# Strassen's seven half products in place of eight for six pairs of blocks in the channel MLP's second batch

## The chip, the cores and the metric

The kernel runs on 1 core of one Trainium2 chip. The metric is the device time of one execution in microseconds (us). Engines are named as in the profile: PE (TensorE matmul) and PEld (its weight loads), DVE (VectorE), ACT (ScalarE), POOL (GpSimd), SP (the queue that issues most DMAs).

## What is computed

Hash-masked attention, a gated convolution block and a last block that mixes with two Fourier transforms and ends in a channel MLP. The change is in that MLP, shown here with the lines around it:

```
X = np.fft.fft(x, axis=1)
X = np.fft.fft(X, axis=2)
mixed = np.real(X).astype(np.float32)
u = x + mixed
mu = np.mean(u, axis=-1, keepdims=True)
var = np.mean((u - mu) ** 2, axis=-1, keepdims=True)
un = (u - mu) / np.sqrt(var + 1e-06)
ch = np.maximum(un @ w_ch1, 0.0) @ w_ch2
return (u + ch).astype(np.float32)
```

There are 2 batches of 768 tokens, 512 channels and 2048 hidden units. All is float32, and w_ch1 and w_ch2 come as float64.

## The kernel before

A float32 product is made of three products on PE: each operand is split into a high and a low part (type F32R), and high x high, low x high and high x low are summed in PSUM. The kernel runs attention, value product, mixing and channel MLP one behind the other; the change is in the last, function channel.

The 2048 hidden units are 16 blocks of 128 units. Step g of the loop (L1398) handles block f = g % 16 of batch g // 16. `first` (L1362) is the first product of a step: 4 chunks of channels x 3 products, over 512 and then over 256 tokens of the 768 (24 matmuls), into PSUM tile pf, of which there are two; behind each of the two pieces ACT writes the ReLU as the high part of `hidden` (L1374) and DVE the low part (L1375). `second` (L1377) multiplies the block's hidden units with its rows of w_ch2: 3 matmuls over 512 channels for each of the 6 tiles of 128 tokens, 18 in all, added up over all blocks in six PSUM tiles acc. Step g runs first(g) and then second(g - 1), so that ACT and DVE work on the hidden units of g meanwhile. `hidden` has two buffers, for even and odd blocks. In the first batch the steps also load and split the weights of later blocks (channel_split); all weights then stay in SBUF as wch[f], four tiles a block: high and low of w_ch1, high and low of w_ch2. In the second batch nothing is loaded, and POOL has no work. The centred tokens of the second batch lie transposed in uth and utl (high and low, 4 chunks of 128 channels x 768 tokens). At steps with 9 <= f < 15 ACT adds the mean back to one tile of u (L1413, 128x512). `result` (L1384) adds u to acc times rstd on DVE and sends the output from SP.

All engines take their instructions in the order in which the code is written (manual_schedule); pools reuse tiles with waits for the last use of each tile.

Of the kernel before, what the change touches and what calls it, by code (L numbers as in the profile page):

```python
# [10 lines left out]
F32 = mybir.dt.float32  # L11
F32R = mybir.dt.float32r
AF = mybir.ActivationFunctionType
ALU = mybir.AluOpType
# [3 lines left out]
P = 128  # L18
B, H, S, D = 2, 8, 768, 64
DM = H * D  # L20
DFF = 2048
NF = DFF // P
# [3 lines left out]
NC = DM // P  # L26
HS = S // 2
# [77 lines left out]
def block_kernel(  # L105
# [4 lines left out]
    nc = tc.nc  # L110

    def f32(ap):
        return ap.bitcast(F32)
# [10 lines left out]
    def pool(es, name, bufs=1, psum=False, side=None):  # L124
        kw = dict(space=bass.MemoryType.PSUM) if psum else {}
        if side:
            kw["side"] = side
        return es.enter_context(tc.tile_pool(name=name, bufs=bufs, reuse_waits="tile", **kw))
# [47 lines left out]
    def run(steps):  # L176
        for x in steps:
            x()
# [5 lines left out]
    g = [gpool.tile([P, NC, S + 1], F32, name=f"g{b}") for b in range(B)]  # L184
# [788 lines left out]
    with ExitStack() as es:  # L973
        ps, late, convs = attention(es)


    u, mu, uth, utl, rstd = [], [], [], [], []
    wq, wch, wraw, wst, wnext = None, [], {}, [], []

    def late_tiles():  # L980
        lpool = pool(ctx, "lpool", side="right")
        for b in range(B):
            u.append(lpool.tile([P, 6, DM], F32, name=f"u{b}"))
            mu.append(lpool.tile([P, 6, 2], F32, name=f"mu{b}"))
        rstd.append(lpool.tile([P, B, 6], F32, name="rstd"))
        uth.append(lpool.tile([P, NC, S], F32R, name="uth"))
        utl.append(lpool.tile([P, NC, S], F32R, name="utl"))

        nonlocal wq
        wq = pool(ctx, "wq", side="right")  # L990
        wst.append(pool(ctx, "wst", 2, side="right"))
        wch.append(channel_tiles(wq, 0))

    def channel_tiles(pl, f):
        return [pl.tile([P, NC, P] if i < 2 else [P, DM], F32R, name=f"w{i}_{f}") for i in range(4)]

    def channel_load(h):

        if h >= 2 * NF:
            return  # L1000
        f, i = divmod(h, 2)
        fs = slice(f * P, (f + 1) * P)
        r = wraw[h] = wq.tile([P, DM], I64, tag=f"raw{i}", name="raw")
        if i:
            nc.sync.dma_start(r, w_ch2[fs, :])
        else:
            nc.sync.dma_start(r.rearrange("p (c f) -> p c f", c=NC), w_ch1[:, fs].rearrange("(c p) f -> p c f", p=P))
# [4 lines left out]
    def channel_steps(h, spare=True):  # L1012
        f, i = divmod(h, 2)
        return from64(channel_words, wraw[h], lambda: wch[f][2 * i : 2 * i + 2], spare=spare)

    def channel_split(h):
        if h < 2 * NF:
            f, i = divmod(h, 2)
            run(channel_steps(h))
            channel_load(h + 2)  # L1020

    def center(b, t):

        st = wst[0].tile([P, 6], F32, tag="st", name="st")
        nc.vector.bn_stats(st, u[b][:, t, :])
        nc.vector.bn_aggr(mu[b][:, t, :], st)
        nc.vector.tensor_scalar(u[b][:, t, :], u[b][:, t, :], mu[b][:, t, 0:1], None, op0=ALU.subtract)

    def spread():
        r = rstd[0]  # L1030
        for b in range(B):
            nc.vector.tensor_scalar(r[:, b, :], mu[b][:, :, 1], 1e-6, None, op0=ALU.add)
        nc.scalar.activation(r, r, AF.Sqrt)
        nc.vector.reciprocal(r, r)

    def u_transpose(b, t, psum):
        pu = psum()
        for c in range(NC):
            nc.tensor.transpose(pu[:, c * P : (c + 1) * P], u[b][:, t, c * P : (c + 1) * P], ident)
        ts_ = slice(t * P, (t + 1) * P)  # L1040
        pv_ = pu.rearrange("p (c t) -> p c t", c=NC)
        nc.scalar.copy(uth[0][:, :, ts_], pv_)
        nc.vector.tensor_tensor(utl[0][:, :, ts_], pv_, f32(uth[0])[:, :, ts_], op=ALU.subtract)
# [299 lines left out]
    def channel(es):  # L1343
        fp = pool(es, "fp")
        psh = pool(es, "psh", 2, psum=True)
        psa = pool(es, "psa", psum=True)
        wch.extend([None] * (NF - 1))
        order = list(range(NF - 1, NF - 5, -1)) + list(range(1, NF - 4))
        for f in order[:4]:
            wch[f] = channel_tiles(fp, f)  # L1350
        hidden = [[fp.tile([P, S], F32R, name=f"hid{n}{i}") for i in range(2)] for n in range(2)]

        for f in order[4:]:
            wch[f] = channel_tiles(fp, f)
        run(wnext)
        channel_load(4)

        def tile_f():
            return psh.tile([P, 512], F32, tag="pf", name="pf")

        def tile_a(t):
            return psa.tile([P, 512], F32, tag=f"acc{t}", name="acc")  # L1362

        def first(g, a):
            f, (hh, hl) = g % NF, hidden[g % 2]
            w1h, w1l = wch[f][:2]
            cs = WIDE[a]
            pf = (tile_a(2 + a) if g == 1 else tile_f())[:, : cs.stop - cs.start]
            n = 0
            for w, x in ((w1h, uth[0]), (w1l, uth[0]), (w1h, utl[0])):  # L1370
                for c in range(NC):
                    nc.tensor.matmul(pf, w[:, c, :], x[:, c, cs], start=n == 0, stop=n == 3 * NC - 1)  # L1372
                    n += 1
            nc.scalar.activation(hh[:, cs], pf, AF.Relu)  # L1374
            nc.vector.scalar_tensor_tensor(hl[:, cs], pf, 0.0, f32(hh)[:, cs], op0=ALU.max, op1=ALU.subtract)  # L1375

        def second(g, t, acc):  # L1377
            f, (hh, hl) = g % NF, hidden[g % 2]
            w2h, w2l = wch[f][2:]
            ts_ = slice(t * P, (t + 1) * P)  # L1380
            for n, (x, w) in enumerate(((hh, w2h), (hh, w2l), (hl, w2h))):
                nc.tensor.matmul(acc, x[:, ts_], w, start=f == 0 and n == 0, stop=f == NF - 1 and n == 2)  # L1382

        def result(b, t, acc):  # L1384

            if t < 3:
                o = wq.tile([P, DM], F32, tag="cv" + "aeg"[t], name="o")
            else:
                if t != 4:
                    both[:] = [wq.tile([P, 2, DM], F32, tag=f"raw{t // 5}", name="o")]  # L1390
                o = both[0][:, t % 2, :]
            nc.vector.scalar_tensor_tensor(
                o, acc, rstd[0][:, b, t : t + 1], u[b][:, t, :], op0=ALU.mult, op1=ALU.add
            )
            nc.sync.dma_start(out[b, t * P : (t + 1) * P, :], o)

        both = []

        last = [tile_a(t) for t in range(2)]
        for g in range(B * NF + 1):  # L1400
            if g < B * NF:
                for a in range(2):
                    first(g, a)
                channel_split(2 * g + 3 if g != 1 else 4)
            if 4 <= g < 10:
                center(1, g - 4)
            elif g == 12:
                spread()
            if g > 0:
                b, f = divmod(g - 1, NF)  # L1410
                if 9 <= f < 15:
                    x = u[b][:, f - 9, :]
                    nc.scalar.activation(x, x, AF.Identity, bias=mu[b][:, f - 9, 0:1])  # L1413
                if f == 0:
                    acc = (last if b == 0 else [tile_a(t) for t in range(2)]) + [tile_a(t) for t in range(2, 6)]
                for t in range(6):
                    if g == NF - 1:
                        for x in ((), (0, 1), (2,), (3,), (4,), (5,))[t]:
                            u_transpose(1, x, tile_f)
                    second(g - 1, t, acc[t])  # L1420
                    if t == 2:
                        channel_split(2 * g + 4 if g > 1 else 5)
                    elif t == 5 and g == 1:
                        channel_split(6)
                    if f == NF - 1:
                        result(b, t, acc[t])

    with ExitStack() as es:
        channel(es)
# [35 lines left out]
```

## Time and profile before

| what | us |
|---|---|
| median of 3 runs | 611.06 (610.6 to 614.76) |
| the profiled execution | 610.95 |
| its span, first to last instruction | 609.1 |
| mean granted clock of TensorE | 0.999 of full speed |

The profile comes from one execution. A busy PE is not a PE at its peak, since the ends of matmuls are modelled and overlap the next start; the pace of PE is read from starts. A number such as L1372 is a line of the kernel before; the code of the change has lines of its own.

### The profile page before, as it was taken

The page shows a single profiled execution, that of the slowest core. Times are in us where ns is not written, and L with a number is a line of the kernel's source. Part 1 is how long each engine was busy: PE and PEld are TensorE (multiplying, and loading weights), DVE is VectorE, ACT ScalarE, POOL GpSimd, SP SyncE. Part 2 cuts the span into 40 slices and gives each one's busy share as a digit, 9 for nine tenths or more (in the row PEclk, how much of TensorE's full clock was granted, in tenths as well). Part 3 has the DMA queues.
Part 4 walks back from the last instruction along what each step waited for, and adds up shares of the span by engine and source line. Part 5 has one row for each costly group of instructions (what it writes and reads, how often), then busy time and mean ns, then how long its engine had stood idle before and what let it go on. Part 6 is the DMA issues. An engine that isn't in the chain of part 4 may idle for free.

```text
span 609.1 us, 10268 instructions
## 1 busy us (share of the span) xinstructions
PE 600.7 (99%) x3711; PEld 537.5 (88%) x3711; DVE 441.4 (72%) x849; ACT 357.7 (59%) x712; POOL 265.3 (44%) x274
## 2 busy tenths in 40 slices
PE   8999999999999999999999999999999999999997
PEld 7899999999999999998989888888888888888885
DVE  4999999999999997998679788988884411110113
ACT  5989999999999997745524455555665011111121
POOL 7251769788888798963341532332330000000000
PEclk9999999999999999999999999999999999999999
DMA  5967776878777712170200243443430200000002
GB/s 133 213 154 165 170 147 164 179 167 189 165 177 178 173 43 57 43 293 2 70 1 9 86 126 127 138 120 123 139 103 1 104 0 1 1 0 1 0 1 104
DMA packets 52556, 62.01 MB, mean 102 GB/s; under 512 B 28704, under 2 KB 39304, under 8 KB 52250
## 3 DMA queue, kind: packets, MB, share of 16 engines
q1 hardware_dynamic: 51770, 57.81, 37.3%
q0 software_dynamic: 432, 3.55, 1.5%
q8 instruction: 29, 0.48, 0.3%
q14 instruction: 21, 0.17, 0.1%
q10 hardware_dynamic: 304, 0.01, 0.0%
HBM read 36.73 MB, written 3.19 MB: 66 GB/s over the span
## 4 chain that ended last, share of the span: by engine, by line
PE 90%; DVE 6%; ACT 2%; issue 1%; DMA 1%; POOL 0%; SPq 0%; ACTq 0%; POOLq 0%
PE pf L1372 21%; PE acc L1382 20%; PE op L629 10%; PE sp L570 10%; PE ptp L606 9%; PE ps L1189 5%; PE ps L222 3%; PE ps L1253 3%; PE ps L1224 1%; PE bp L456 1%; PE late L222 1%; PE ptp L714 1%; PE early L222 1%; DVE ptl L618 1%; PE idle L369 1%
## 5 line engine op out<-in xcount | busy, mean ns | idle before, releaser
L1382 PE MATMUL acc<-w,hid 128*128 128x512 f32 x576 | 137.4, 391 | 0.0
L1382 PEld LDWEIGHTS acc<-w,hid 128*128 128x128 f32 x576 | 105.5, 188 | 20.1
L1375 DVE SCALAR_TENSOR_TENSOR hid<-pf,hid 128x512 fp32r<-128x512 f32 (+1 forms) x62 | 33.4, 556 | 120.6 <-ACT hid L1374 120.6
L1372 PE MATMUL pf<-uth,w 128*128 128x512 f32 (+1 forms) x496 | 97.2, 337 | 0.1
L1374 ACT ACTIVATE hid<-pf 128x512 fp32r<-128x512 f32 (+1 forms) x62 | 28.9, 488 | 114.9 <-PE pf L1372 114.9
L581 DVE TENSOR_SCALAR_CACHE_REDUCE sd<-sp 128x768 f32<-128x768 f32 x96 | 91.0, 948 | 4.8 <-PE sp L570 3.1
L618 DVE TENSOR_TENSOR ptl<-ptp,pth 128x768 fp32r<-128x768 f32 x96 | 91.5, 953 | 2.3 <-ACT pth L614 2.0
L570 PE MATMUL sp<-qk 128*128 128x512 f32 (+1 forms) x384 | 91.1, 359 | 1.7 <-DVE sd L581 0.8
L1372 PEld LDWEIGHTS pf<-uth,w 128*128 128x128 f32 x496 | 78.8, 188 | 15.6 <-DVE hid L1375 1.8
L588 ACT ACTIVATE sd<-sd,nm 128x768 f32<-128x768 f32 x96 | 90.5, 942 | 1.5 <-DVE sd L581 1.5
L614 ACT CAST pth<-ptp 128x768 fp32r<-128x768 f32 x96 | 77.4, 806 | 13.6 <-PE ptp L714 5.7
L162 POOL TENSOR_TENSOR w<-cv 128x512 fp32r<-128x512 f32 x31 | 40.4, 1302 | 89.0 <-DVE cv L157 74.5
L606 PE MATMUL ptp<-ident,sd 128*128 128x128 f32 x576 | 78.5, 272 | 0.2 <-ACT sd L588 0.2
L629 PE MATMUL op<-ptl,v 128*128 128x256 f32 x288 | 73.3, 284 | 0.2 <-DVE ptl L618 0.2
L629 PE MATMUL op<-pth,v 128*128 128x256 f32 x288 | 73.3, 282 | 0.0
L606 PEld LDWEIGHTS ptp<-ident,sd 128*128 128x128 f32 x576 | 65.8, 140 | 1.1 <-ACT sd L588 0.5
L570 PEld LDWEIGHTS sp<-qk 128*128 128x128 f32 x384 | 58.2, 189 | 8.3 <-DVE sd L581 1.6
L629 PEld LDWEIGHTS op<-pth,v 128*128 128x128 f32 x288 | 54.1, 188 | 4.1
L629 PEld LDWEIGHTS op<-ptl,v 128*128 128x128 f32 x288 | 54.1, 188 | 0.6 <-DVE ptl L618 0.4
L1372 PE MATMUL pf<-utl,w 128*128 128x512 f32 (+1 forms) x248 | 53.1, 335 | 0.0
L241 POOL TENSOR_TENSOR g<-g,conv_tmp 128x768 f32<-128x768 f32 x27 | 46.5, 1723 | 1.6
L149 ACT ACTIVATE cv<-cv,col 128x512 int32<-128x512 int32 x32 | 23.2, 725 | 40.4 <-DVE cv L146 40.4
(214 smaller groups left out, 984.2 us busy)
## 6 DMA issues: line engine op xcount, KB each, us to landing
raw<-in_moe_w_ch_dram SPq DMA_DIRECT2D x32, 512.0 KB
qk<-ht SPq DMA_DIRECT2D x60, 192.0 KB
qk<-lt SPq DMA_DIRECT2D x30, 192.0 KB
rqk<-in_q_dram SPq DMA_DIRECT2D x16, 192.0 KB
rqk<-in_k_dram SPq DMA_DIRECT2D x16, 192.0 KB
rv<-in_v_dram SPq DMA_DIRECT2D x8, 384.0 KB
out_dram<-o SPq DMA_DIRECT2D x12, 256.0 KB
xm<-xc SPq DMA_DIRECT2D x15, 192.0 KB
```

Source lines behind the costliest of these rows:

```text
L162: nc.gpsimd.tensor_tensor(dst()[1], fold(g.bitcast(F32)), fold(e.bitcast(F32)), op=ALU.mult)
L241: nc.gpsimd.tensor_tensor(dst, dst, tmp, op=ALU.add)
L570: nc.tensor.matmul(sp[:, cs], q2[i][:, m, qi * P : (qi + 1) * P], k2[i][:, m, cs], start=m == order[0], stop=m == order[1])
L581: nc.vector.tensor_scalar(sd[n], sp, CLAMP, None, op0=ALU.min, op1=ALU.min, accum_out=st[p]["nm"][:, n % 12 : n % 12 + 1],)
L588: nc.scalar.activation(sd[n], sd[n], AF.Exp, bias=st[p]["nm"][:, i : i + 1], scale=-1.0, accum_out=st[p]["sums"][:, i : i + 1],)
L606: nc.tensor.transpose(tp[:, r // 3, c0 : c0 + P], sd[n][:, r * P : (r + 1) * P], ident)
L614: nc.scalar.copy(p_parts(n)[0], tp)
L618: nc.vector.tensor_tensor(lo, tp, f32(ho), op=ALU.subtract)
L629: nc.tensor.matmul(po[kb], v3[:, r, c0 : c0 + P], pt[kb][x][:, r, :], start=r == 0 and x == 0, stop=r == R - 1 and x == 1,)
L1372: nc.tensor.matmul(pf, w[:, c, :], x[:, c, cs], start=n == 0, stop=n == 3 * NC - 1)
L1375: nc.vector.scalar_tensor_tensor(hl[:, cs], pf, 0.0, f32(hh)[:, cs], op0=ALU.max, op1=ALU.subtract)
L1382: nc.tensor.matmul(acc, x[:, ts_], w, start=f == 0 and n == 0, stop=f == NF - 1 and n == 2)
```

## The change

Steps 0 to 19 (the first batch and blocks 0 to 3 of the second) keep first and second. Then come six pairs of blocks, q = 2 to 7, with blocks 2q (e) and 2q + 1 (o). The first product of a pair is a 2x2 matrix product of halves: block e or o, upper or lower half of the channels (2 chunks of 128), left or right half of the tokens (384). Eight products of halves become seven (P1 to P7 in the order in which `seven` runs them), each of 6 matmuls of 384 tokens, of sums of weights and sums of tokens. The sums of tokens are made once (token_sums, DVE and ACT, in steps 17 to 19; tiles from batch 0's u, from raw0 and raw1 and from weight tiles no longer needed). The sums of weights are made for each pair (weight_sums, POOL and ACT), into the w_ch1 tiles of the pair two earlier. The seven products are added up in a new SBUF tile `between` (parts m, t1, t2), by one copy on ACT and seven additions on DVE, and four ReLU pieces of 384 tokens follow on ACT and four low parts on DVE. The second products of the pair before (two blocks, 36 matmuls) run between the products. The additions of the mean move behind seven(4) to seven(6), two tiles a time.

```diff
+        between = fp.tile([P, 3, HS], F32, name="between")
...
+        def token_sums(step):
...
+        def sum_tiles(q):
+            return [wch[f][i] for f in (2 * q - 4, 2 * q - 3) for i in range(2)]
+
+        def weight_sums(q):
+            e, o = wch[2 * q], wch[2 * q + 1]
+            tt = nc.gpsimd.tensor_tensor
+            we, wo = (wq.tile([P, NC, P], F32, tag=f"cv{x}", name="wsum") for x in "ae")
+            t = wq.tile([P, 2, 2, P], F32, tag="cvg", name="wsum")
+            tiles = sum_tiles(q)
+
+            def parts(i, x):
+                nc.scalar.copy(tiles[i][:, upper], x)
+                tt(tiles[i][:, lower], x, f32(tiles[i])[:, upper], op=ALU.subtract)
+
+            tt(wo, f32(o[0]), f32(o[1]), op=ALU.add)
+            tt(t[:, 0], wo[:, upper], wo[:, lower], op=ALU.add)
+            tt(we, f32(e[0]), f32(e[1]), op=ALU.add)
+            tt(t[:, 1], t[:, 0], we[:, upper], op=ALU.subtract)
+            parts(0, t[:, 0])
+            parts(1, t[:, 1])
+            tt(t[:, 0], we[:, lower], t[:, 1], op=ALU.subtract)
+            parts(3, t[:, 0])
+            tt(t[:, 1], we[:, upper], wo[:, upper], op=ALU.subtract)
+            parts(2, t[:, 1])
+
+        def seven(q, seconds):
...
+            def product(w, x):
+                ps = tile_f()[:, :HS]
+                n = 0
+                for i, j in ((0, 0), (1, 0), (0, 1)):
+                    for c in range(2):
+                        nc.tensor.matmul(ps, w[i][c], x[j][c], start=n == 0, stop=n == 5)
+                        n += 1
+                return ps
+
+            def high(par, cs, x):
+                nc.scalar.activation(hidden[par][0][:, cs], x, AF.Relu)
+
+            def low(par, cs, x):
+                nc.vector.scalar_tensor_tensor(
+                    hidden[par][1][:, cs], x, 0.0, f32(hidden[par][0])[:, cs], op0=ALU.max, op1=ALU.subtract
+                )
+
+            nc.scalar.copy(m, product(weights(e, 0), tokens(0, left)))
+            tt(t1, product(sums(2), token_sum(2)), m, op=ALU.add)
+            for t in range(3):
+                seconds(t)
+            tt(m, product(weights(e, 2), tokens(2, left)), m, op=ALU.add)
+            high(0, left, m)
+            low(0, left, m)
+            tt(t2, product(sums(3), token_sum(3)), t1, op=ALU.add)
+            for t in range(3, 5):
+                seconds(t)
+            ps = product(sums(1), token_sum(1))
+            tt(t1, ps, t1, op=ALU.add)
+            tt(m, ps, t2, op=ALU.add)
+            tt(t2, product(weights(o, 2), token_sum(4)), t2, op=ALU.add)
+            seconds(5)
+            high(1, right, m)
+            low(1, right, m)
+            high(1, left, t2)
+            tt(t1, product(sums(4), tokens(2, right)), t1, op=ALU.add)
+            low(1, left, t2)
+            high(0, right, t1)
+            low(0, right, t1)
...
-        for g in range(B * NF + 1):
-            if g < B * NF:
-                for a in range(2):
-                    first(g, a)
-                channel_split(2 * g + 3 if g != 1 else 4)
+        for g in range(NF + 4):
+            for a in range(2):
+                first(g, a)
+            channel_split(2 * g + 3 if g != 1 else 4)
...
+            if g > NF:
+                token_sums(g - NF - 1)
+            if g == NF + 2:
+                weight_sums(2)
+        left_over = [NF + 3]
+        for q in range(2, NF // 2):
+            seven(q, lambda t: [second(g, t, acc[t]) for g in left_over])
+            left_over = [NF + 2 * q, NF + 2 * q + 1]
+            if q + 1 < NF // 2:
+                weight_sums(q + 1)
+            if 4 <= q < 7:
+                for t in (2 * q - 8, 2 * q - 7):
+                    x = u[1][:, t, :]
+                    nc.scalar.activation(x, x, AF.Identity, bias=mu[1][:, t, 0:1])
+        for t in range(6):
+            for g in left_over:
+                second(g, t, acc[t])
+            result(1, t, acc[t])
```

What stands in the engines' queues around the border of two pairs. ACT of the kernel before, in the middle of the second batch (hid00 and hid10 are the high parts of even and odd blocks, u1 the second batch's u); a bracket names the engines that an instruction waits for:

```order
L1374 ACTIVATE hid00_4774<-pf_6563 128x512 [waits DVE_49,PE_49]
L1374 ACTIVATE hid00_4774<-pf_6578 128x256 [waits DVE_49,PE_49]
L1413 ACTIVATE u1_4163<-u1_4163,mu1_4164 128x512
L1374 ACTIVATE hid10_4776<-pf_6612 128x512 [waits DVE_49,PE_49]
L1374 ACTIVATE hid10_4776<-pf_6627 128x256 [waits DVE_49,PE_49]
```

ACT of the change, from the copy of P1 of pair 2 to the first ReLU of pair 3 (w0_2, w1_2, w1_3 and w0_3 are the w_ch1 tiles of blocks 2 and 3, which take the weight sums of pair 3; wsum is the sum on POOL):

```order
L1506 COPY between_4778<-pf_6314 128x384 [waits DMASW2_49,DVE_49,PE_49]
L1499 ACTIVATE hid00_4774<-between_4778 128x384 [waits DVE_49]
L1499 ACTIVATE hid10_4776<-between_4778 128x384 [waits DVE_49,PE_49,Activation_49]
L1499 ACTIVATE hid10_4776<-between_4778 128x384 [waits DVE_49]
L1499 ACTIVATE hid00_4774<-between_4778 128x384 [waits DVE_49]
L1456 CAST w0_2_4783<-wsum_6399 128x256 [waits Pool_49]
L1456 CAST w1_2_4784<-wsum_6399 128x256 [waits Pool_49]
L1456 CAST w1_3_4788<-wsum_6399 128x256 [waits Pool_49]
L1456 CAST w0_3_4787<-wsum_6399 128x256 [waits Pool_49]
L1506 COPY between_4778<-pf_6414 128x384 [waits PE_49,Activation_49]
L1499 ACTIVATE hid00_4774<-between_4778 128x384 [waits DVE_49]
```

The four casts of the weight sums stand between the last ReLU piece of a pair, which needs that pair's P7, and the copy of the next pair's P1.

PE of the change at the same border: P7 of pair 2 (weight w1_1), P1 of pair 3 (weights w0_6, w1_6), P2 of pair 3 (weight w1_2, the second sum), and the second products of blocks 4 and 5:

```order
L1494 MATMUL pf_6386<-uth_4166,w1_1_4780 128x384 [waits DVE_49]
L1494 MATMUL pf_6386<-uth_4166,w1_1_4780 128x384 x3
L1494 MATMUL pf_6386<-utl_4167,w1_1_4780 128x384 x2
L1494 MATMUL pf_6414<-uth_4166,w0_6_4799 128x384 [waits DVE_49]
L1494 MATMUL pf_6414<-uth_4166,w0_6_4799 128x384
L1494 MATMUL pf_6414<-uth_4166,w1_6_4800 128x384 x2
L1494 MATMUL pf_6414<-utl_4167,w0_6_4799 128x384 x2
L1494 MATMUL pf_6422<-tsum_6188,w1_2_4784 128x384 [waits DVE_49,Activation_49]
L1494 MATMUL pf_6422<-tsum_6188,w1_2_4784 128x384
L1494 MATMUL pf_6422<-tsum_6188,w1_2_4784 128x384 [waits Pool_49]
L1494 MATMUL pf_6422<-tsum_6188,w1_2_4784 128x384 x3
L1385 MATMUL acc_6156<-w2_4_4793,hid00_4774 128x512
```

P2 stands six matmuls behind P7 and waits for the cast of its weight on ACT and, from its third matmul on, for POOL.

POOL of the change, the ten operations of pair 3's weight sums (before, POOL has nothing here):

```order
L1459 TENSOR_TENSOR wsum_6398<-w0_7_4803,w1_7_4804 128x512
L1460 TENSOR_TENSOR wsum_6399<-wsum_6398 128x256 [waits Pool_49]
L1461 TENSOR_TENSOR wsum_6397<-w0_6_4799,w1_6_4800 128x512
L1462 TENSOR_TENSOR wsum_6399<-wsum_6399,wsum_6397 128x256 [waits Pool_49]
L1457 TENSOR_TENSOR w0_2_4783<-wsum_6399,w0_2_4783 128x256 [waits PE_49,Activation_49]
L1457 TENSOR_TENSOR w1_2_4784<-wsum_6399,w1_2_4784 128x256 [waits Activation_49]
L1465 TENSOR_TENSOR wsum_6399<-wsum_6397,wsum_6399 128x256 [waits Pool_49]
L1457 TENSOR_TENSOR w1_3_4788<-wsum_6399,w1_3_4788 128x256 [waits PE_49,Activation_49]
L1467 TENSOR_TENSOR wsum_6399<-wsum_6397,wsum_6398 128x256
L1457 TENSOR_TENSOR w0_3_4787<-wsum_6399,w0_3_4787 128x256 [waits PE_49,Activation_49]
```

The first four wait for nothing but POOL itself; from the fifth on they alternate with ACT's casts.

## Rows read from the trace of the kernel before

**Rows 1.** The page's busy times of each engine.

```profile
PE 600.7 (99%) x3711; PEld 537.5 (88%) x3711; DVE 441.4 (72%) x849; ACT 357.7 (59%) x712; POOL 265.3 (44%) x274
```

**Rows 2.** Chain that ended last, in order of time: start, us, what.

```profile
493.50 4.17 PE pf L1372 x24
497.68 4.09 PE acc L1382 x18
...
596.88 6.83 PE acc L1382 x30
...
605.14 0.75 DVE o L1392
```

**Rows 3.** Windows of one step: length, PE, PEld, DVE, ACT, POOL busy (instructions), PEclk, DMA.

```profile
485.20:493.50 8.30, 8.30 (x44) 7.03 (x43) 1.12 (x2) 0.98 (x2) 0.00 (x0) 1.00 0.00 0
```

**Rows 4.** PE in order of time, 252.5 to 261.5: start, us, operation.

```profile
252.80 0.87 PE L222 MATMUL ps<-xh,wvh 128*128 128x384 f32 x4
...
261.15 0.52 PE L222 MATMUL ps<-xsh,wvh 128*128 128x384 f32 x2
```

**Rows 5.** Groups by shape, whole span: out<-in xcount | busy, mean ns | idle before.

```profile
L581 DVE TENSOR_SCALAR_CACHE_REDUCE sd<-sp 128x768 f32<-128x768 f32 x96 | 91.0, 948 | 4.8 <-PE sp L570 3.1
L162 POOL TENSOR_TENSOR w<-cv 128x512 fp32r<-128x512 f32 x31 | 40.4, 1302 | 89.0 <-DVE cv L157 74.5 <-ACT w L169 8.9 <-DVE rstd L1032 2.9
L169 ACT CAST w<-cv 128x512 fp32r<-128x512 f32 x32 | 19.9, 622 | 4.5 <-PE ps L1253 4.3 <-DVE cv L156 0.2
L1090 POOL TENSOR_TENSOR gl<-gt,gh 128x384 fp32r<-128x384 f32 x16 | 15.8, 1012 | 14.5 <-ACT gh L1087 14.5
L1413 ACT ACTIVATE u<-u,mu 128x512 f32<-128x512 f32 x12 | 8.6, 716 | 0.0
L1087 ACT CAST gh<-gt 128x384 fp32r<-128x384 f32 x16 | 7.4, 524 | 0.0
L231 DVE TENSOR_TENSOR late<-late,g 128x384 f32<-128x384 f32 x4 | 2.2, 557 | 0.0
```

**Rows 6.** In order of time, step 19: start, us, operation [idle before <-releaser].

```profile
493.34 2.03 PE L1372 MATMUL pf<-uth,w 128*128 128x512 f32 x8
495.21 1.09 PE L1372 MATMUL pf<-utl,w 128*128 128x512 f32 x4
...
496.34 0.60 ACT L1374 ACTIVATE hid<-pf 128x512 fp32r<-128x512 f32 x1 [6.51 <-PE pf L1372]
496.97 0.69 DVE L1375 SCALAR_TENSOR_TENSOR hid<-pf,hid 128x512 fp32r<-128x512 f32 x1 [6.68 <-ACT hid L1374]
497.51 4.26 PE L1382 MATMUL acc<-w,hid 128*128 128x512 f32 x18
497.71 0.38 ACT L1374 ACTIVATE hid<-pf 128x256 fp32r<-128x256 f32 x1 [0.78 <-PE pf L1372]
```

**Rows 7.** In order of time, three places where POOL or PE waits.

```profile
276.40 0.94 ACT L1087 CAST gh<-gt 128x384 fp32r<-128x384 f32 x2
277.07 1.99 POOL L1090 TENSOR_TENSOR gl<-gt,gh 128x384 fp32r<-128x384 f32 x2 [8.19 <-ACT gh L1087]
...
348.10 1.29 POOL L162 TENSOR_TENSOR w<-cv 128x512 fp32r<-128x512 f32 x1 [2.87 <-DVE cv L157]
349.44 0.53 PEld L1372 LDWEIGHTS pf<-uth,w 128*128 128x128 f32 x3 [0.48 <-POOL w L162]
...
398.63 2.13 PE L1372 MATMUL pf<-uth,w 128*128 128x512 f32 x8
400.59 1.09 PE L1372 MATMUL pf<-utl,w 128*128 128x512 f32 x4
```

**Rows 8.** Line L1082, DVE subtraction of two SBUF operands: ns min/median/max.

```profile
L1082 DVE TENSOR_TENSOR gt<-g x8: 544/554/1358, 275.0 to 287.8; 128x384 f32<-128x384 f32 x8
```

**Rows 9.** Windows after the last matmul, columns as in rows 3.

```profile
607.00:608.00 1.00, 0.00 (x0) 0.00 (x0) 0.00 (x0) 0.00 (x0) 0.00 (x0) 1.00 0.47 182
608.00:609.10 1.10, 0.00 (x0) 0.00 (x0) 0.00 (x0) 0.00 (x0) 0.00 (x0) 0.70 0.00 0
```

More of the change, by code (lines that the diff above doesn't have):

```diff
@@ L978, in block_kernel @@
     wq, wch, wraw, wst, wnext = None, [], {}, [], []
+    lpool = None
     def late_tiles():
+        nonlocal lpool
         lpool = pool(ctx, "lpool", side="right")
         for b in range(B):
-            u.append(lpool.tile([P, 6, DM], F32, name=f"u{b}"))
+            u.append(lpool.tile([P, 6, DM], F32, tag=f"u{b}", name=f"u{b}"))
             mu.append(lpool.tile([P, 6, 2], F32, name=f"mu{b}"))
@@ L1397, in channel, with parts @@
         both = []
-        last = [tile_a(t) for t in range(2)]
-        for g in range(B * NF + 1):
-            if g < B * NF:
-                for a in range(2):
-                    first(g, a)
-                channel_split(2 * g + 3 if g != 1 else 4)
+        left, right = slice(0, HS), slice(HS, S)
+        upper, lower = slice(0, 2), slice(2, NC)
+        tsum = {}
+        def token_sums(step):
+            h, l = uth[0], utl[0]
+            tt = nc.vector.tensor_tensor
+            def parts(name):
+                high, low = tsum[name][:2]
+                x = tsum[name][2]
+                for c in range(2) if isinstance(high, list) else [slice(None)]:
+                    nc.scalar.copy(high[c] if isinstance(high, list) else high, x[:, c])
+                    tt(
+                        low[c] if isinstance(low, list) else low, x[:, c],
+                        f32(high[c] if isinstance(high, list) else high), op=ALU.subtract,
+                    )
+            if step == 0:
+                t1 = wq.tile([P, 2, HS], F32, tag="raw0", name="t1")
+                t3 = wq.tile([P, 2, HS], F32, tag="raw1", name="t3")
+                t2 = between[:, 0:2, :]
+                tt(t3, f32(h)[:, upper, right], f32(l)[:, upper, right], op=ALU.add)
+                tt(t1, t3, f32(h)[:, upper, left], op=ALU.subtract)
+                tt(t1, t1, f32(l)[:, upper, left], op=ALU.subtract)
+                tt(t2, f32(h)[:, lower, right], f32(l)[:, lower, right], op=ALU.add)
+                tt(t3, t2, t3, op=ALU.subtract)
+                tt(t2, t2, t1, op=ALU.subtract)
+                x = lpool.tile([P, 4, 2, HS], F32R, tag="u0", name="tsum")
+                tsum[1] = x[:, 0], x[:, 1], t1
+                tsum[2] = x[:, 2], x[:, 3], t2
+                w = [wch[f][i][:, :HS] for f in range(2) for i in (2, 3)]
+                tsum[3] = w[:2], w[2:], t3
+                tsum[4] = h[:, upper, right], l[:, upper, right], t1
+                parts(1)
+            elif step == 1:
+                t1, t2 = tsum[1][2], tsum[2][2]
+                tt(t1, f32(h)[:, lower, left], t2, op=ALU.subtract)
+                tt(t1, t1, f32(l)[:, lower, left], op=ALU.add)
+                parts(2)
+                parts(3)
+            else:
+                parts(4)
@@ new lines, in seven, with weights, sums, tokens @@
+        def seven(q, seconds):
+            e, o = wch[2 * q], wch[2 * q + 1]
+            h, l = uth[0], utl[0]
+            tiles = sum_tiles(q)
+            m, t1, t2 = (between[:, i, :] for i in range(3))
+            tt = nc.vector.tensor_tensor
+            def weights(w, c0):
+                return [[x[:, c0 + c, :] for c in range(2)] for x in w[:2]]
+            def sums(i):
+                return [[tiles[i - 1][:, 2 * x + c, :] for c in range(2)] for x in range(2)]
+            def tokens(c0, cs):
+                return [[x[:, c0 + c, cs] for c in range(2)] for x in (h, l)]
+            def token_sum(i):
+                return [[x[c] if isinstance(x, list) else x[:, c, :] for c in range(2)] for x in tsum[i][:2]]
+            def product(w, x):
[11 more added lines that the diff above has]
+                    hidden[par][1][:, cs], x, 0.0, f32(hidden[par][0])[:, cs], op0=ALU.max, op1=ALU.subtract
+                )
+            nc.scalar.copy(m, product(weights(e, 0), tokens(0, left)))
[20 more added lines that the diff above has]
+            low(0, right, t1)
```

## The prediction

> **What bounds the kernel now.** I read the busy times first: PE is busy for 99% of the span, and apart from its own weight loads nothing is for more than 72% [rows 1]. The chain of waits in order of time shows what that means here: through the second batch it goes back and forth between 24 matmuls of `first` in 4.17 us and 18 of `second` in 4.09 us, with no other engine between them, up to one `result` on DVE at the end [rows 2]. The window of one step says why nothing else shows: in 8.3 us DVE works 1.12 us, ACT 0.98 us, POOL not at all, and the granted clock is 1.00 [rows 3]. So each microsecond of matmuls that goes is a microsecond of the total, and so is each that PE waits. The profiled execution took 610.95 us, 1.85 more than its span; the median is 611.06, so a sum made against the one stands for the other within 0.1 us. A measurement of this kernel can tell about 1%, 6.1 us, from no change.
>
> **Matmuls.** The first products of a pair take 2 x 4.17 = 8.34 us [rows 2]. In their place come 7 products of 6 matmuls of 384 tokens. The value product has such matmuls back to back: 48 of them from 252.80 to 261.15, 0.174 us each [rows 4]. The same comes out of `first` itself: 12 matmuls of 512 and 12 of 256 are 9216 columns in 4.17 us, 384 of which are 0.174 us. So 42 x 0.174 = 7.31 us, a gain of 1.03 us a pair and 6.2 us for six. The 36 second products of a pair are the same before and after.
>
> **Weight sums.** The first four POOL operations of a pair need nothing of the pair before (2 of 512 columns at 1.30 us [rows 5], 2 of 256) and are long done. What counts begins with the casts: ACT works in order, its casts stand behind the pair's last ReLU, this behind P7, and the next pair's P2 waits for the second of them and for POOL's subtraction after it. P2 stands only six matmuls, 1.04 us, behind P7. From the start of P1 (time 0):
> - P7 is seen on another engine 0.20 us later, as ACT starts 0.20 after PE went on at 497.51 [rows 6]. DVE adds P7 to t1: PSUM and SBUF, 384 columns, 0.56 us [rows 5]. End 0.76.
> - ACT's last ReLU piece, 384 columns from SBUF, 0.03 us later, as between ACT and DVE [rows 6], 0.52 us as the nearest cast [rows 5]: end 1.31.
> - Two casts of 256 columns. At 512 columns one takes 0.62, at 384 0.52 us [rows 5], so about 0.43; two back to back take 0.1 us less than their sum (0.94 for two of 0.52 [rows 7]), and the first overlaps the ReLU in that way too. Ends 1.64 and 1.97.
> - POOL starts 0.15 us after a cast: of two casts from 276.40, the first done at 276.92, POOL at 277.07 [rows 7]. From 1.79 it makes two subtractions of 256 columns. The trace has none of that width: from 512 columns (1.30 us) and 384 (1.01 us) [rows 5] the line gives 0.72 us; half the wide one is 0.65, and the row of 384, 1.01, is the other bound. I take 0.72: end 3.23.
> - PE goes on 0.05 us after POOL (349.39 to 349.44 [rows 7]) and about 0.1 us is lost since the weights are not loaded ahead (8 matmuls took 1.96 us after a wait at 398.63 [rows 7], else 1.87 [rows 6]): 3.38. Then the last four matmuls of P2: 4.08.
>
> P1 and P2 back to back would end at 2.09. So PE loses 2.0 us in two gaps (before P2, and after two matmuls of it), for each of the pairs 3 to 7: 5 x 2.0 = 10.0 us. With the bounds of the subtraction it is 1.85 to 2.6 a pair, 9.2 to 13.0. Nothing hides it, as all second products that could stand behind P2 in PE's order. Pair 2 is spared: its weight sums are written in step 18, a step ahead.
>
> **Token sums.** DVE has eleven operations of 768 columns in steps 17 to 19, at about 0.95 us [rows 5], and two half as wide: 11.6 us in three steps, beside 1.1 us of low parts each [rows 3], in 24.8 us. They fit, but the low parts of step 18 come late. Their pf tiles are wanted again a whole `second`, 4.09 us, after they fill [rows 2], which covers it. If that cover fails, pair 2 starts up to 1 us late; I take 0.
>
> **Putting the seven together.** DVE has 11 operations of about 0.55 us a pair, ACT 5: some 9 us in 17. With two pf tiles, a product waits for the reading of the last but one; 12 to 18 second products or another product lie between, enough for one or two additions. One place is tight: the copy of P1 stands on ACT behind the fourth cast, which needs four more POOL operations, and behind the two additions of a mean (0.72 us each [rows 5]) in pairs 5 to 7. It ends about 7.1, with the means 8.4; P3 wants that tile at 4.08 + 4.09 = 8.17. I take 0.2 us for each of three, 0.6. The moved additions of the mean cost nothing else: ACT is idle in most of a step [rows 3]. The output DMAs stay where they were.
>
> **The end.** After P7 of pair 7 no products cover the hidden units. The second product of block 15 needs its left low part, which DVE makes behind the addition of P7, 0.76 + 0.56 = 1.3 us after P7. PE would want it after five matmuls of 0.227 us, at 1.1: 0.2 us lost, 0.4 if DVE is a little late; I take 0.3. The last `result` still ends the chain [rows 2].
>
> **Sum.** -6.2 + 10.0 + 0.6 + 0.3 = +4.7: 610.95 + 4.7 = 615.7 us, 0.8% slower. With the low ends (9.2, 0, 0.2) it is 614.1, with the high ends (13.0, 0.9, 0.4 and the 1 us of pair 2) 620.0; I put less of the chance near the top, since it has a subtraction of 256 columns cost as much as one of 384.
>
> **Rivals.**
> - *No wait.* If the sums of weights are there in time, only -6.2 + 0.3 is left: 605.1 us, not slower, and just at the bound of what counts as faster. For it speaks that POOL is idle in this stage [rows 3]. Against it stands the order on ACT: the casts can't start before P7 is added. 0.06.
> - *DVE and POOL in each other's way.* DVE subtractions with two SBUF operands take 0.55 us, but 1.36 where POOL was at work [rows 8]. The low parts of the hidden units are such operations, and one of them stands just ahead of the addition of P7, one beside the first POOL subtraction. A collision in the path costs up to 0.8 us: 5 x 0.8 = 4.0, 619.7 us, slower. By my times POOL is idle when the first comes, and the second overlaps by some 0.1 us. From 0.3 us a pair on the change is slower by over 1%. 0.22. The Trainium skill ("SBUF — State Buffer", Who interferes with whom) says that a DVE instruction with two SBUF inputs contends with a GpSimd instruction that reads SBUF; the trace agrees, by the 1.36 us.
> - *The clock falls.* PE now stands still twice a pair. If the clock fell to 1.2 GHz there, the 18 second products behind P2 would take 8.2 us and not 4.1: 5 x 4.1 = 20 us, 636 us. Against it: after the last matmul, at 605, the granted clock is still 1.00 from 607 to 608 and falls only then [rows 9]; my gaps are about 1 us each. 0.03. The Trainium skill ("TensorE: Matmul & The Clock Gate", Part 1: The HAM clock gate) has an idle TensorE fall back to its lower clock, the rule that speaks most against waits like these; that gaps as short as mine do it, no row here shows.
>
> **How the numbers follow.** The forecast holds 0.69, with its own range from 614 to 618.5. Of it about 0.09 lies above 617.1, where slower by over 1% begins. Slower: 0.09 + 0.18 of the second rival's 0.22 + 0.03 = 0.30. The first rival's 605.1 lies just inside 1%, and with matmuls that gain a little more it lies outside: 0.04 of its 0.06 is faster. Within 1%: the rest, 0.66. The range ends above with the high ends and the second rival, at 620.0; below it goes to 611.0, where PE would lose half of what I worked out, 1.05 us a pair (-6.2 + 5.25 + 0.9). The first and third rival, and a little beyond the second, are left out.
>
> **What would show it.** In the changed profile PE's weight loads of P2 should wait for ACT's cast and for POOL's subtraction, about 1 us each, five times, and hardly for anything else; the distance from one P1 to the next should be 7.31 + 8.18 + 2.0 = 17.5 us against 16.5 for two steps before; six matmuls of a product should start within 1.05 us; the clock should stay at 1.00. It is wrong if P2 doesn't wait (the order on ACT doesn't bind), if DVE's low parts take 1.3 us on the path, or if the clock falls.

## The result, and the profile after

| | before | with the change |
|---|---|---|
| median of 19 runs, us | 611.1 | 615.81 |
| lowest to highest, us | 610.26 to 614.76 | 614.9 to 618.07 |
| the profiled execution, us | 610.95 | 614.9 |
| its span, us | 609.1 | 613.1 |

The ratio is 1.0078 (95% interval 1.0069 to 1.0088): 0.8% slower, as 615.7 us had said.

The busy times of each engine after the change, to be read against [rows 1]:

```profile
PE 597.4 (97%) x3675; PEld 536.7 (88%) x3675; DVE 479.1 (78%) x904; ACT 371.6 (61%) x747; POOL 316.8 (52%) x334
```

PE has less to do, and yet the end is later: its share of the span fell from 99 to 97%. Where it stands still shows in the chain of waits that ended last, here from P3 of pair 3 to P3 of pair 4 (start, us, what; L1494 are the products of halves, L1385 the second products), to be read against [rows 2]:

```profile
520.54 2.12 PE pf L1494 x12
522.66 2.76 PE acc L1385 x12
525.42 2.10 PE pf L1494 x12
527.52 1.39 PE acc L1385 x6
528.91 1.06 PE pf L1494 x6
...
530.00 0.57 DVE between L1524
...
530.65 0.52 ACT hid L1499
531.17 0.30 ACT w L1456
...
531.54 1.50 POOL w L1457 x2
...
533.09 0.96 PE pf L1494 x4
534.05 4.12 PE acc L1385 x18
538.18 2.12 PE pf L1494 x12
```

The chain leaves PE behind P7 and goes over DVE (adding P7), ACT (the last ReLU, the first cast) and POOL (two subtractions) back to the last four matmuls of P2. From 520.54 to 538.18, one pair, are 17.64 us; the two steps of the kernel before that it replaces took 16.5. The same place in order of time:

```profile
529.80 0.86 PE L1494 MATMUL pf<-uth,w 128*128 128x384 f32 x4
530.00 0.56 DVE L1524 TENSOR_TENSOR between<-pf,between 128x384 f32<-128x384 f32 x1 [0.16 <-PE pf L1494]
...
530.65 0.52 ACT L1499 ACTIVATE hid<-between 128x384 fp32r<-128x384 f32 x1 [0.99 <-DVE between L1524]
531.08 0.69 ACT L1456 CAST w<-wsum 128x256 fp32r<-128x256 f32 x2
...
531.54 1.49 POOL L1457 TENSOR_TENSOR w<-wsum,w 128x256 fp32r<-128x256 f32 x2 [8.12 <-ACT w L1456]
531.83 0.30 PEld L1494 LDWEIGHTS pf<-tsum,w 128*128 128x128 f32 x2 [1.14 <-ACT w L1456]
...
533.09 0.96 PE L1494 MATMUL pf<-tsum,w 128*128 128x384 f32 x4 [0.65 <-POOL w L1457]
```

POOL had stood idle for 8.12 us before its subtraction, with its sums ready, until ACT made the casts. Right behind P1, which takes 1.05 us, P2 would begin at 530.85. It begins at 531.83, stops after two matmuls, and goes on at 533.09. From P1 to the second products are 4.09 us (529.80 to 533.89). The waits of PE's weight loads from 470 us on (us in total, times, longest):

```profile
PEld pf L1494 <- ACT w L1456: 5.6, 5, 1.1
PEld pf L1494 <- POOL w L1457: 4.8, 5, 1.0
...
PEld acc L1385 <- DVE hid L1502: 0.4, 1, 0.4
```

Five waits for the cast, five for the subtraction, and one at the end for the low part of block 15: no other. So in each of the pairs 3 to 7 PE stands still twice, for about 0.8 and 0.65 us.

### The profile page after: what moved, and what is told of

It reads as the page before. It is cut to its first block, busy times and chain, and to the rows that moved or that the text cites. A ratio compares the mean times of both kernels' runs of the same rounds, so it can differ in the third digit from the quotient of the medians.

```text
span 613.1 us, 10401 instructions
## 1 busy us (share of the span) xinstructions
PE 597.4 (97%) x3675; PEld 536.7 (88%) x3675; DVE 479.1 (78%) x904; ACT 371.6 (61%) x747; POOL 316.8 (52%) x334
## 4 chain that ended last, share of the span: by engine, by line
PE 87%; DVE 6%; ACT 2%; POOL 2%; DMA 1%; issue 1%; SPq 1%; ACTq 0%; POOLq 0%
PE acc L1385 20%; PE pf L1375 12%; PE op L629 10%; PE sp L570 10%; PE ptp L606 9%; PE pf L1494 6%; PE ps L1191 5%; PE ps L222 3%; PE ps L1255 3%; PE ps L1226 1%; PE bp L456 1%; PE late L222 1%; PE ptp L714 1%; POOL w L1457 1%; PE early L222 1%; DMA rqk<-in_k_dram 1%
## 5 line engine op out<-in xcount | busy, mean ns | idle before, releaser
L1385 PE MATMUL acc<-w,hid 128*128 128x512 f32 x576 | 139.3, 392 | 0.0
L1385 PEld LDWEIGHTS acc<-w,hid 128*128 128x128 f32 x576 | 106.1, 188 | 20.3 <-DVE hid L1502 0.4
L1375 PE MATMUL pf<-uth,w 128*128 128x256 f32 (+1 forms) x304 | 59.8, 338 | 0.1
L1375 PEld LDWEIGHTS pf<-uth,w 128*128 128x128 f32 x304 | 48.2, 188 | 9.8 <-DVE hid L1378 1.2
L1457 POOL TENSOR_TENSOR w<-wsum,w 128x256 fp32r<-128x256 f32 x24 | 18.7, 789 | 60.7 <-ACT w L1456 60.7
L1499 ACT ACTIVATE hid<-between 128x384 fp32r<-128x384 f32 x24 | 11.9, 521 | 57.2 <-PE acc L1385 33.8
L657 POOL TENSOR_TENSOR xm<-xc,xm 64x768 f32<-64x768 f32 (+1 forms) x18 | 30.0, 1668 | 26.8 <-DMA xm<-xc 16.1
```

## The experiments

Each was run beside the kernel before on the same chip; ratios are to the kernel before and have their 95% interval. The expectations name two rivals: that products of halves are slow by themselves with only two PSUM tiles, and that DVE and POOL hold each other up.

**The second weight sum first.** Two lines of weight_sums change places:

```diff
-            parts(0, t[:, 0])
             parts(1, t[:, 1])
+            parts(0, t[:, 0])
```

> The second weight sum, the one P2 needs, is cast and subtracted before the first. Theory (P2 waits for its weight sum, which stands on ACT behind the pair's last ReLU and on POOL behind one subtraction of another sum): one POOL subtraction of 0.75 us leaves the path of each of the five pairs, so 5 x 0.75 = 3.75 us less than the change, 612.1 us, and P2's second gap goes from about 0.65 to nearly nothing. Rival 1 (the 2 us a pair are the pace of split products with only two PSUM tiles): no difference, 615.8. Rival 2 (DVE's two-operand subtractions and POOL block each other on the path): within 1 us of the change, 615 to 616, since the same operations meet.

614.87 us, ratio 1.0064 (1.0039 to 1.0089): 0.9 us less than the change, not 3.75. P2's second gap did shrink, from 0.65 to 0.27 us, and the way from P1 to the second products from 4.09 to 3.41. But in pairs 5 to 7 another wait took its place. P3 of pair 6 of this run:

```profile
572.05 1.33 ACT L1569 ACTIVATE u<-u,mu 128x512 f32<-128x512 f32 x2
...
573.29 0.45 ACT L1506 COPY between<-pf 128x384 f32<-128x384 f32 x1
...
573.80 0.64 PEld L1494 LDWEIGHTS pf<-uth,w 128*128 128x128 f32 x4 [0.83 <-ACT between L1506]
573.80 0.96 PE L1494 MATMUL pf<-uth,w 128*128 128x384 f32 x4 [0.41 <-ACT between L1506]
```

P3 needs the PSUM tile of P1, whose copy stands on ACT behind the fourth cast and two additions of a mean. In the change P3 came later by what P2 lost, and just missed this wait. So two of five pairs gain 0.68 us, 1.4 in all; from P1 of pair 2 to the last result this run's profile has 106.92 us (502.65 to 609.57) and that of the change 108.36 (500.68 to 609.04). By its time alone the run looks like the second rival's; only the two gaps and the new wait speak for the theory, so the next run takes that wait away.

**The same, with the means at the end.**

```diff
-            if 4 <= q < 7:
-                for t in (2 * q - 8, 2 * q - 7):
-                    x = u[1][:, t, :]
-                    nc.scalar.activation(x, x, AF.Identity, bias=mu[1][:, t, 0:1])
         for t in range(6):
+            x = u[1][:, t, :]
+            nc.scalar.activation(x, x, AF.Identity, bias=mu[1][:, t, 0:1])
             for g in left_over:
```

> As in the run with the second weight sum first, and the six additions of the mean stand at the end, one ahead of each output tile, and not behind pairs 4 to 6. Theory (the swap gave 0.68 us in pairs 3 and 4 and nothing in pairs 5 to 7, since there P3 then waited for the copy of P1, which stands on ACT behind the fourth cast and two additions of a mean): with the means gone P3 waits in no pair, the five pairs each gain 0.68 us, 5 x 0.68 = 3.4 us less than the change, 612.4 us. Rival (the swap reaches only so far for another reason, such as the fourth cast itself): the time stays near that of the swap alone, 614.4 to 615.

612.29 us, ratio 1.0025 (1.0014 to 1.0037). It is the expected 612.4. The waits of PE's weight loads in this run:

```profile
PEld pf L1494 <- ACT w L1456: 4.1, 5, 0.8
PEld pf L1494 <- POOL w L1457: 3.0, 5, 0.6
```

All five pairs gain, and P3 waits for the copy in none.

**The weight sums written early.** weight_sums(q + 1) is called inside seven(q):

```diff
             tt(t2, product(sums(3), token_sum(3)), t1, op=ALU.add)
+            sums_next()
             for t in range(3, 5):
```

> The weight sums of the next pair are written behind the addition of P4, in the middle of a pair, so that ACT's four casts stand ahead of the ReLU pieces that need P5 to P7. Nothing else differs. Theory: the wait of P2 goes, 5 x 2.0 us: 605.8 us, faster than before by 0.9%, and no wait of PE over 0.3 us in a pair. Rival 1 (pace of split products): 615.8. Rival 2 (DVE and POOL in each other's way): the collisions move with POOL, and the time stays above 609.

606.77 us, ratio 0.9928 (0.9913 to 0.9943). P2 waits for its weights in no pair. Most of what is over the expected 605.8 comes from pair 2, and the expectation that PE waits nowhere over 0.3 us failed by it. The chain of this run there:

```profile
509.22 1.75 PE pf L1494 x10
...
511.02 0.74 POOL w L1457
511.76 0.70 POOL wsum L1467
...
512.80 0.53 ACT hid L1499
513.33 0.02 issue
513.35 0.78 DVE hid L1502
514.12 0.48 DVE between L1525
...
514.74 1.28 PE pf L1494 x6
```

Pair 2 has only half as many second products, so the four casts, which alternate with POOL, aren't done when its last ReLU pieces come. The low part and the addition of P7 behind them are late, and P2 of pair 3 waits 0.65 us for P7's PSUM tile.

**The casts on POOL.** The sums stay where the change has them:

```diff
             def parts(i, x):
-                nc.scalar.copy(tiles[i][:, upper], x)
+                pool_copy(tiles[i][:, upper], x)
```

> The weight sums stay where they are in the code, but POOL makes the four casts and not ACT, so that they stand behind no ReLU. POOL then has 14 operations a pair, some 10 us of 15.5. Theory (the order on ACT makes the wait): the wait goes as in the run with the sums written early, 605.8 us. Rival 1 (pace of split products): 615.8. Rival 2 (DVE and POOL in each other's way): POOL works longer and meets DVE more often, 612 or more.

605.34 us, ratio 0.9903 (0.9888 to 0.9918), the fastest kernel here: 0.97% under before. Nothing but the engine of the casts was changed. In the run before this one they stayed on ACT, but stood earlier, and the wait was gone too. So it is their place on ACT, behind the last ReLU, that made the wait. A pair of this run:

```profile
527.42 3.14 PE pf L1494 x18
530.56 4.12 PE acc L1385 x18
534.68 2.12 PE pf L1494 x12
536.80 2.76 PE acc L1385 x12
539.57 2.10 PE pf L1494 x12
541.67 1.39 PE acc L1385 x6
543.05 3.14 PE pf L1494 x18
```

P7, P1 and P2 follow each other as 18 matmuls in 3.14 us. The pair takes 15.63 us against 17.64: the wait was 2.0 us.

**No weight sums.** weight_sums(q + 1) is left out, which leaves four of the seven products of pairs 3 to 7 with weights of an earlier pair; the rest is the same.

```diff
-            if q + 1 < NF // 2:
-                weight_sums(q + 1)
```

> The weight sums of pairs 3 to 7 are left out: P2, P4, P5 and P7 of these pairs take the weights of the pair two earlier as they are. This is the price of seven products, additions and ReLU pieces without the sums. Theory: 605.8 us, the same as with the sums written early, which would then cost nothing; the gain over before is what 42 matmuls of 384 tokens save, 5.8 to 6.2 us less some 0.3 at the end. Rival 1 (pace of split products): 615.8, since the sums were not the cause.

606.34 us, ratio 0.9918 (0.9899 to 0.9937), its four runs from 605.06 to 607.14. Within its interval that is the time with the casts on POOL, and in the profiles a pair takes 15.63 us in either: sums that don't wait in ACT's queue cost nothing that shows.

**One more subtraction on POOL.** The subtraction of the first weight sum, which stands ahead of the one that P2 waits for, is made twice:

```diff
             parts(0, t[:, 0])
+            tt(tiles[0][:, lower], t[:, 0], f32(tiles[0])[:, upper], op=ALU.subtract)
             parts(1, t[:, 1])
```

> The change with POOL's first subtraction of a pair (the low part of the first weight sum) made twice, so that one more operation of 256 columns, 0.75 us, stands ahead of the subtraction that P2 waits for. Theory (POOL's queue ahead of P2 is on the path of each of the pairs 3 to 7): 5 x 0.75 = 3.75 us more than the change, 619.5 us; P2's second gap grows by 0.75 us in each pair. Rival (the place of POOL's work doesn't count, since the split products set the pace): 615.8.

624.87 us, ratio 1.0237 (1.0218 to 1.0256): 9.1 us over the change and not 3.75. P2's second gap grew as expected, from 0.65 to 1.45 us. The chain (pairs 4 and 6) and the windows of pair 4 (columns as in [rows 3]) show what else came:

```profile
536.60 5.62 PE acc L1385 x18
...
576.51 4.12 PE acc L1385 x18
```

```profile
534.00:535.00 1.00, 0.05 (x1) 0.00 (x0) 0.00 (x0) 0.00 (x0) 0.96 (x2) 1.00 0.00 0
535.00:536.00 1.00, 0.50 (x3) 0.50 (x4) 0.00 (x0) 0.00 (x0) 1.00 (x2) 1.00 0.00 0
536.00:537.00 1.00, 1.00 (x5) 0.91 (x4) 0.00 (x0) 0.41 (x1) 0.48 (x2) 0.60 0.06 16
537.00:538.00 1.00, 1.00 (x4) 0.81 (x3) 0.00 (x0) 0.00 (x0) 1.00 (x2) 0.50 0.00 0
538.00:539.00 1.00, 1.00 (x4) 0.72 (x4) 0.08 (x1) 0.78 (x2) 0.48 (x2) 0.50 0.00 0
539.00:540.00 1.00, 1.00 (x5) 0.82 (x4) 0.47 (x1) 0.00 (x0) 1.00 (x2) 0.69 0.00 0
```

The 18 second products behind P2 took 5.62 us in place of 4.12, since the clock was granted at half (1.2 GHz) from 537 to 539 and for parts of the microseconds before and behind. In pairs 4, 5 and 7 it fell so: the second products took 5.62, 5.70 and 5.18 us, and the four matmuls ahead of them 0.13 and 0.5 us more in pairs 4 and 7. That is 4.8 us in all, and with five gaps that are 0.8 us longer, 4.0, it is 8.8 of the 9.1.

**The same with PE kept at work.** In pairs 3 to 7, 12 matmuls that nobody reads go into P2's PSUM tile ahead of P2:

```diff
-            def product(w, x):
+            def product(w, x, fill=0):
                 ps = tile_f()[:, :HS]
+                for n in range(fill):
+                    nc.tensor.matmul(ps, e[n % 2][:, 0, :], h[:, 0, left], start=True, stop=True)
                 n = 0
...
-            tt(t1, product(sums(2), token_sum(2)), m, op=ALU.add)
+            tt(t1, product(sums(2), token_sum(2), 12 if q > 2 else 0), m, op=ALU.add)
```

> As in the run with one more POOL subtraction, but PE makes 12 matmuls of 384 tokens whose results are overwritten, just ahead of P2 in pairs 3 to 7 (2.1 us, into P2's own PSUM tile). P2's weights come as late as in that run, so PE's wait for useful work is the same or a little longer; what differs is that PE isn't idle. Theory (of that run's 9.1 us over the change 3.75 are the operation, and the rest is the clock, which was granted at half for some 3 to 4 us in three of five pairs): the clock stays at full speed, and the time is 615.8 + 3.75 = 619.6 us, at most 620.5. Rival (the rest is a second wait, and the clock has nothing to do with it): 624 to 625, as in that run.

619.72 us, ratio 1.0135 (1.0119 to 1.0152), as expected. The chain and a window of pair 4 in this run:

```profile
535.50 0.97 PE pf L1497 x4
536.46 4.12 PE acc L1385 x18
```

```profile
530.00:540.00 10.00, 9.53 (x50) 8.45 (x49) 2.70 (x5) 3.26 (x8) 5.77 (x8) 1.00 0.01 2
```

P2 goes on at 535.50 as in the run before, but the clock stays at 1.00 and the second products take 4.12 us. Useless matmuls in a wait saved 5.2 us. The two runs were made on different chips, but the kernel before took 610.71 us beside the one and 610.9 beside the other; the mean clock was 0.988 to 0.991 in all four runs of the one and 0.999 or 1.000 in all four of the other.

**The change itself with PE kept at work**, 5 such matmuls in its first gap:

```diff
-            tt(t1, product(sums(2), token_sum(2)), m, op=ALU.add)
+            tt(t1, product(sums(2), token_sum(2), 5 if q > 2 else 0), m, op=ALU.add)
```

> The change with 5 matmuls of 384 tokens ahead of P2 in pairs 3 to 7 (0.9 us, in the first of the two gaps), whose results are overwritten. Theory (the runs of the change that lie near 617 to 618 us are those in which the clock fell once in a gap; their mean clock is 0.996 or 0.997, that of the others 0.998 to 1.000): with less idle time the clock doesn't fall, every run has a mean clock of 0.999 or more, none lies above 617 us, and the median is 615.4 to 615.8. Rival (the scatter of the change has another cause): some of the runs again lie at 617 us and more.

615.81 us, ratio 1.0079 (1.0063 to 1.0094), six runs from 615.62 to 617.1. The highest has a mean clock of 0.999, so the expectation that none lies above 617 failed; another run has 0.998, where 0.999 or more was expected. In the 19 runs of the change, six have a mean clock of 0.997 or less and take 617.2 us on average, thirteen have 0.998 or more and take 615.6. The 1.6 us between them are what one fall cost in the run with one more subtraction. That the clock falls now and then in the change too fits this, but there is no trace of such a run, and the filling didn't settle it.

## Why the prediction was right

The time was right for the reason given: P2 waits for a cast that stands on ACT behind the last ReLU of the pair before, and for POOL behind it. Three runs that take this wait away (casts on POOL, sums earlier, no sums) end at 605 to 607 us. The two rivals of the expectations had 615.8 and at least 609 for the first two of them, so neither of them makes the wait. That the sum came within 0.1 us is in part luck, since two of its terms were wrong and nearly cancel. Point by point:

- *Matmuls.* Foreseen: 7.31 us for the products of a pair, a gain of 1.03. Without waits, as with the casts on POOL, they take 2.12 + 2.10 + 3.14 = 7.36 us, a gain of 0.98 against [rows 2]. The second products, taken as unchanged, rose from 8.18 to 4.12 + 2.76 + 1.39 = 8.27 us, in smaller groups between the products. For six pairs the gain is 5.9 - 0.5 = 5.4 us, 0.8 less than foreseen.
- *The wait.* Foreseen 4.08 us from P1 to the second products, measured 4.09; 2.0 us a pair, 10.0 in all, as 17.64 - 15.63 shows. The operation that the trace before had not, POOL's subtraction of 256 columns, took about 0.75 us (two in 1.49), where the line through 512 and 384 columns had given 0.72.
- *The copy of P1.* Foreseen 0.6 us in pairs 5 to 7; the change loses nothing there. The copy of pair 5 ends at 555.37 and P3's weights load from 555.46 on: P3 was late enough. The swap, which made P2 earlier, brought this wait out. This term was wrong by 0.6 and, by luck, hid that the gain in matmuls was put 0.8 too high.
- *Token sums* and pair 2: no wait, as foreseen. *The end*: the last 36 second products took 8.45 us, where 36 at the pace of [rows 2] are 8.19, so 0.3 as foreseen.

The second batch, from the second products of the first batch's block 15 to the last result, took 137.10 us (471.94 to 609.04) against 132.26 (472.88 to 605.14): 4.8 us more, for 4.7 foreseen. That the profiled execution is only 3.95 us longer comes from ahead of that, where the same code was 0.94 us earlier. The medians, 19 runs each, differ by 4.7 us.

The prediction's rivals: *No wait* fell with the gaps. *DVE and POOL in each other's way* does happen, but off the path. In the change:

```profile
521.32 1.29 POOL L1461 TENSOR_TENSOR wsum<-w,w 128x512 f32<-128x512 f32 x1
...
522.69 0.73 POOL L1462 TENSOR_TENSOR wsum<-wsum 128x256 f32<-128x256 f32 x1
522.78 1.05 DVE L1502 SCALAR_TENSOR_TENSOR hid<-between,hid 128x384 fp32r<-128x384 f32 x1 [0.59 <-ACT hid L1499]
523.76 0.54 DVE L1513 TENSOR_TENSOR between<-pf,between 128x384 f32<-128x384 f32 x1
...
526.33 0.85 PE L1494 MATMUL pf<-uth,w 128*128 128x384 f32 x4
```

A low part that takes 0.56 us elsewhere takes 1.05 beside POOL's sum of 0.73, so 0.5 us more, where the prediction had up to 0.8. But the addition behind it still ends at 524.30, and P6, which wants that PSUM tile, starts at 526.33. The Trainium skill's rule on two SBUF operands ("SBUF — State Buffer", Who interferes with whom), that a DVE instruction with two of them contends with a POOL instruction that reads SBUF, holds here by that row. *The clock* was granted in full through the whole stage of the profiled run, as foreseen. But its fall was nearer than the chance of 0.03 said: 0.8 us more in one gap brought it down in three of five pairs. Where it fell it cost about 1.6 us and not the 4.1 of the prediction, since it came back while the second products ran.

## What to carry to other kernels

When an engine that works in order prepares operands for the next tile, look at what stands ahead of that work in its queue, not at whether the engine is idle: POOL was idle for 8 us and ready, and ACT was busy for 21 of the 84 us from 516 to 600, but four casts written behind a late ReLU cost 10 us, more than the 5.4 that the seven products gave. Work that needs nothing of the current tile belongs ahead of the work that does, or on another queue; here one line that moves the casts to POOL turns 0.8% slower into 1.0% faster (605.34 us). And take out one wait only after asking which comes next: the swap's gain was eaten in three of five pairs by a copy that had just been on time.

## What the runs showed of the hardware that was not expected

The clock falls on much shorter idling than the end of the kernel before suggests [rows 9]: with PE idle for 0.8 and 1.45 us and two matmuls between, it fell to half in three of five places, when PE had already gone on, and came back while it worked, at a price of about 1.6 us each time (4.8 for three). With gaps of 0.8 and 0.65 us, as in the change, the profiled run shows none. The Trainium skill ("TensorE: Matmul & The Clock Gate", Part 1: The HAM clock gate) has an idle TensorE fall back to the lower clock. The run with PE kept at work agrees that idling is the cause, by 619.72 against 624.87 us; that gaps as short as these bring it down, only the runs here show.
